# Attention and Fourier mixing on one core: start, last blocks and the turn of the row ends rearranged

## The chip, the core and the metric

The kernel runs on one core of one Trainium2 chip. The metric is the device time of one execution in microseconds (us), lower is better. Durations of single instructions come from a profile of one execution. In the profile PE is TensorE, PEld its weight loads, DVE is VectorE, ACT is ScalarE, POOL is GpSimd and SP is SyncE, which only issues DMAs here. A "q" behind an engine's name (SPq) marks its queue.

## What is computed

Two independent parts, laid side by side along the last axis of the output (2048 rows, 2 x 1024 columns, fp32):

```python
# A: attention with 32 heads of 32, one shared key and value head
q = (A_x @ wq) as [heads, rows, 32]; k = A_x @ wk; v = A_x @ wv
p = softmax(q @ k.T / sqrt(32)); a = concat_heads(p @ v) @ wo
# B: Fourier mixing, real part
re = B_x @ hid_re.T; im = B_x @ hid_im.T
b = seq_re @ re - seq_im @ im
out = concatenate([a, b], axis=-1)
```

The inputs have 2048 rows of 1024 columns, the sequence transform is 2048 x 2048. The inputs of A are scaled up, so that scores are large and the products must be precise.

## The kernel before

**Products in two parts.** Nearly every matrix product of 128 x 128 by 128 x 512 is done three times on operands rounded to fp32r: a left operand `m` is split into `mh` (rounded) and `ml` (the rest), a right operand `r` into `rh` and `rl`, and `rh*mh + rl*mh + rh*ml` is summed in PSUM. For each operand the steps are: load by SP, combine if it is a sum of several, round (`cast`, line 174), subtract the rounded part (`lo`, line 244). `cast` runs on ACT and the subtraction on DVE until the first 48 products are issued (`START`, line 563), later both on POOL. Two lines of such items, `RL` for right and `ML` for left operands (class `Line`, line 139; lines 257 and 258), have rings of buffers and due times counted in products: `pump` takes each step when the product it is due for is near, `step(k)` takes one step, `force(item)` takes all that an item still needs. A step of the program is an issue only; each engine works through its own queue in order, and waits where data or a buffer is not there.

**Fill.** A `Group` (line 77) is 24 such products (8 right blocks, 2 left items) into one PSUM bank named `psb`. `pos["fill"]` counts the products issued. `take(n)` (line 352) issues the next n. The groups are, in this order: the projections to q (32 groups, `q_group`), B's first stage, B's second stage (products as a scheme with fewer multiplications, so that operands are sums, `PRODUCTS`), and the output projection with wo. They are the "fill" that is put between the steps of attention, so that PE has work while ACT and DVE do the softmax.

**Attention.** 32 units (block of 512 rows times group of 4 heads). For each, 32 score steps (`score_step`, line 696): two products into a PSUM tile `pss` of 2 banks, DVE takes the negative row maximum into `nm`, ACT the exponential with its row sum. A unit's row ends are then formed in the next unit's first steps: `lse_1` (DVE, maxima), `lse_1b` (ACT, a small exponential), `lse_2` (DVE, sums and reciprocal), `lse_3` (PE turns the 48 columns of row ends into rows in a `psb` bank, DVE copies them to `mt`), `lse_4` (SP writes two rows into the unit's `qst` and one to memory). The table `LSE` and `TURN` (lines 712 and 713) say at which step. 12 steps behind, `expo` (line 655) forms the turned scores of the unit with these rows in the product, into PSUM tile `pst`, and ACT their exponential `p`; every eighth step `pv` (line 664) multiplies with the values in a `psb` bank.

**Order.** Every engine keeps the program's order (class `Ordered`), all DMAs go through SP's queue, and `level` (line 764) spreads the fill evenly over the 1024 steps from the point `PRO` that is reached after the opening.

**The opening** (lines 715 to 755). Three products of zeros (`v`, just cleared by DVE) into `pst`; then the first block of x: SP loads its 8 pieces, and behind the first of them ML's pump loads, rounds and subtracts the first two blocks of wq; then the 8 pieces of x are rounded and subtracted in turn. Keys and values are formed by `kv_pair` in fp32; `kst` holds the keys in three parts plus two rows of ones, and is cleared by two DVE memsets at lines 118 and 119. Between the two `kv_pair` and behind them stand three groups of fill (`take(24)` each), then the score steps begin, 7 products of fill behind each.

**The end** (lines 787 to 822). The last 8 groups are the last block of rows: for each the first 21 products (`first_part`), and the three with the last unit's result (`last_block`, line 337), which comes last. The first four groups have their 21 products done in the four halves of two `pss` tiles, then their last blocks in a row; the other four follow one by one in `psb`. Each group's `post` copies the bank with DVE into a buffer `qh` and `store` sends it to the output from SP's queue, `BEHIND` = 9 products later in program order.

[...]

Of the kernel before, what the change touches and what calls it, by code (L numbers as in the profile page):

```python
# [8 lines left out]
F32 = mybir.dt.float32  # L9
F32R = mybir.dt.float32r  # L10
AF = mybir.ActivationFunctionType
# [5 lines left out]
P = 128  # L17
# [4 lines left out]
W = 512  # L22
NG = 8
NQ = 4
# [63 lines left out]
def tile_kernel(ctx: ExitStack, tc, xT, wq, wkv, wo, xbT, wT, cT, out):  # L88
    nc = tc.nc
    te = Ordered(tc, nc.tensor)  # L90
    act = Ordered(tc, nc.scalar)
    dve = Ordered(tc, nc.vector)
    gp = Ordered(tc, nc.gpsimd)
    sp = Ordered(tc, nc.sync)
    scale = float(DH) ** -0.5

    def pool(stack, name, bufs, **kw):
        kw.setdefault("reuse_waits", "tile")
        return stack.enter_context(tc.tile_pool(name=name, bufs=bufs, **kw))
# [15 lines left out]
    kst = keep.tile([P, S], F32R, name="kst")  # L115
    v = keep.tile([P, NC, DH], F32, name="v")
    dve.memset(v, 0.0)
    dve.memset(kst[96:P, :].bitcast(F32), 0.0)
    dve.memset(kst[96:98, :].bitcast(F32), 1.0)

    ps_s = pool(ctx, "ps_s", 2, space=PSUM)
    ps_t = pool(ctx, "ps_t", 1, space=PSUM)
    ps_b = [pool(ctx, f"ps_b{i}", 1, space=PSUM) for i in range(2)]
# [8 lines left out]
    op = pool(ctx, "op", 3, side="right")  # L132
    hp = pool(ctx, "hp", 1, side="right")

    def move(q, to, of):
        q.dma_start(to.bitcast(F32), of.bitcast(F32))


    class Line:
# [22 lines left out]
        def pump(self):  # L162
            for k in range(4):
                while self.may(k) and self.items[self.n[k]].due - self.lead[k] <= pos["fill"]:
                    self.step(k)
# [92 lines left out]
    ML = Line(NM0, NM, (52, 36, 27, 21), load_m, comb, hi_m, lo)  # L258
# [42 lines left out]
    def at(p, f):  # L301
        k = len(later)
        while k and later[k - 1][0] > p:
            k -= 1
        later.insert(k, (p, f))

    def run_later():
        while later and later[0][0] <= pos["fill"]:
            later.pop(0)[1]()

    def soon(f):

        if pos["fill"] <= START:
            f()
        else:
            at(pos["fill"] + BEHIND, f)

    def store(to, of, key=None):
        def go():
            move(sp, to, of)  # L320
            if key:
                ready.add(key)
        soon(go)
# [4 lines left out]
    def bank(name, open_=False):  # L328

        b = 1 - cur["bank"] if cur["bank"] is not None else int(used[1] < used[0])  # L330
        cur["at"] += 1
        used[b] = cur["at"]
        if open_:
            cur["bank"] = b
        return ps_b[b].tile([P, W], F32, name=name)
# [10 lines left out]
    def product(g, ps, j):  # L346
        c, w = divmod(j, 3)
        l, r = g.left[c // 4], g.right[c]
        a = (l.lo if w == 2 else l.hi)[:, c % 4]
        te.matmul(ps[:g.rows], a, r.lo if w == 1 else r.hi, start=j == 0, stop=j == g.n - 1)  # L350

    def take(n):
        for _ in range(n):
            if cur["group"] >= len(groups):
                return
            g = groups[cur["group"]]
            j = pos["fill"] - g.at
            if j == 0:
                cur["ps"] = bank("psb", True)
            if j % 3 == 0:  # L360
                RL.force(g.right[j // 3])
            if j % 12 == 0:
                ML.force(g.left[j // 12])
            product(g, cur["ps"], j)
            pos["fill"] += 1
            if j == g.n - 1:
                cur["group"] += 1
                assert all(hasattr(it, "done") for it in g.ys)
                g.post(cur["ps"])
                cur["at"] += 1  # L370
                used[cur["bank"]] = cur["at"]
                cur["bank"] = None
                if g.ys:
                    at(pos["fill"] + 2 * BEHIND, lambda n=len(g.ys): yused.__setitem__(0, yused[0] + n))
            pump()
            run_later()
# [14 lines left out]
    def x_set(b):  # L391
        return [Item([(lambda c=c: xT[b, c], 1)]) for c in range(ND)]
# [148 lines left out]
    def o_left(b, t, q):  # L541
        g1 = min(q * 4 + 4, NQ * NG - 1 - b * NG)

        def src():
            assert all(("o", b, g) in ready for g in range(q * 4, g1)), (b, t, q)
            return [d[b][q * 4:g1, :, t * P:(t + 1) * P].rearrange("g p c -> p g c") for d in (oh_d, ol_d)]
        return Item(None, pre=src)

    def o_group(b, t, e, ws):
        def post(ps):  # L550
            oo = op.tile([P, W], F32, name="qh")
            dve.tensor_copy(oo, ps)
            r0 = b * W + t * P
            store(out[r0:r0 + P, e * W:(e + 1) * W], oo)
        return Group([o_left(b, t, q) for q in range(2)], ws, post)


# [3 lines left out]
    sets = [x_set(b) for b in range(NQ)]  # L561
    start = [q_group(0, g, sets[0]) for g in range(2)]
# [8 lines left out]
    pp = pool(ctx, "pp", 9)  # L571
# [62 lines left out]
    def lse_3(u):  # L634
        aside()
        pm = bank("psb")
        te.transpose(pm[:3 * NC, :P], nm[u][:, 3:6].rearrange("p a b -> p (a b)"), ident)
        mt = sm.tile([3 * NC, P], F32, name="mt")
        dve.tensor_copy(mt, pm[:3 * NC, :P])
        cur["at"] += 1  # L640
        lse[u] = mt
# [54 lines left out]
    def score_step(s):  # L696

        if s < total:
            u, r = divmod(s, SU)
            if r == SU - 6 and u + 1 < len(units):  # L700
                open_unit(u + 1)
        if SU <= s < SU * (len(units) + 1) and s % SU == TURN:
            lse_3((s - SU) // SU)
# [4 lines left out]
        if 0 <= u < len(units):  # L708
            for f in LSE.get(e, ()):
                f(u)  # L710

    TURN = 6
    LSE = {1: (lse_1,), 2: (lse_1b,), 4: (lse_2,), 8: (lse_4,)}

    zeros = v[:, :, :].rearrange("p a b -> p (a b)")
    for _ in range(3):
        te.matmul(ps_t.tile([P, 2, W], F32, name="pst")[:, 0], zeros[:, :P], zeros, start=True, stop=True)
    room = [t[:, k] for t in [pp.tile([P, 2, W], F32, name="p") for _ in range(9)] for k in range(2)]
    room += [hp.tile([P, W], F32, name=f"h{k}") for k in range(8)]
    room += [t[:, k].bitcast(F32) for t in [qsp.tile([P, 4, W], F32R, name="qst") for _ in range(2)] for k in range(4)]  # L720
# [2 lines left out]
    def load_x(b):  # L723
        for c in range(ND):
            sp.dma_start(xs[b][c], xT[b, c])
            if b < 2:
                sets[b][c].t = [xs[b][c]]
            if b == 0 and c == 0:
                ML.pump()

    load_x(0)
    for it in sets[0]:
        RL.force(it)
    wkv_t = onp.tile([P, W], F32, name="ov")
    sp.dma_start(wkv_t, wkv.rearrange("p a b -> p (a b)"))
# [8 lines left out]
    take(24)  # L744
    open_unit(0)
    kv_pair((2, 3), xs[2:])
    take(24)
    for s in range(SU + LEAD):
        score_step(s)
        take(7)  # L750
# [51 lines left out]
            pos["fill"] += 1  # L802
            pump()

    s0, s1 = (ps_s.tile([P, 2 * W], F32, name="pss") for _ in range(2))
    banks = [s0[:, :W], s0[:, W:], s1[:, :W], s1[:, W:]]
    for g, ps in zip(last[:4], banks):
        first_part(g, ps)
    for t, (g, ps) in enumerate(zip(last[:4], banks)):
# [2 lines left out]
        pump()  # L812
        run_later()
    for t, g in enumerate(last[4:]):
        ps = ps_b[t % 2].tile([P, W], F32, name="psb")
        first_part(g, ps)
        last_block(g, ps, t, hi7, lo7)
        pos["fill"] += 3
        pump()
        run_later()  # L820
# [36 lines left out]
```

## Time and profile before

| | us |
|---|---|
| median of three runs | 2773.06 (2770.75 to 2773.42) |
| the profiled execution | 2775.04 |
| its span, first to last instruction | 2773.1 |
| PE busy | 2756.9 (99%) |
| ACT busy | 2169.8 (78%) |
| POOL busy | 1648.2 (59%) |
| DVE busy | 1606.3 (58%) |

All instructions carry one line number, that of a helper, so they are told apart by the tiles they write and read (`out<-in`). A row of the timeline is: start, duration, engine, operation, tiles, shape, number of merged instructions, and in brackets the idle time of the engine just before and what ended it. The shown durations of products overlap, since they are pipelined; the distance from start to start tells the rate. "Granted clock" is the share of full speed that TensorE was given. A list of waits has: who waited, for whom, us in total, times, longest.

### The profile page before, as it was taken

The numbers are of one execution on the slowest core, as the hardware profiler recorded it, in microseconds if no ns is written. First come the engines' busy times: TensorE is split into PE (matmuls) and PEld (weight loads), VectorE is DVE, ScalarE is ACT, GpSimd is POOL, SyncE is SP. The second block draws the span as 40 slices with busy tenths as digits, with TensorE's granted clock in tenths as the row PEclk, the third lists the DMA queues.
The fourth block names the chain that finished last, engine by engine and source line by source line (L and its number), as shares of the span: only waits on it lengthen the run. The fifth ranks groups of instructions, "written<-read, shape, count | busy, mean of one in ns | idle before, by whom it ended". The sixth has DMA issues, their size and how long they took to land.

```text
span 2773.1 us, 39970 instructions
## 1 busy us (share of the span) xinstructions
PE 2756.9 (99%) x13870; PEld 1924.6 (69%) x13870; DVE 1606.3 (58%) x1836; ACT 2169.8 (78%) x3126; POOL 1648.2 (59%) x1618
## 2 busy tenths in 40 slices
PE   9999999999999999999999999999999999999999
PEld 6766676767767676776767676766776767676667
DVE  5766666666666665555556555555555555555411
ACT  3588888888888888888888888878888888888740
POOL 4755525666535547767786576798888885640110
PEclk9999999999999999999999999999999999999999
DMA  7544335675676555555463354565565552554455
GB/s 262 187 132 127 115 104 182 225 235 180 213 238 198 176 165 165 156 161 146 136 200 105 121 174 135 166 199 161 161 190 152 167 161 84 162 163 138 129 165 173
DMA packets 302329, 458.01 MB, mean 165 GB/s; under 512 B 31024, under 2 KB 96048, under 8 KB 302128
## 3 DMA queue, kind: packets, MB, share of 16 engines
q1 hardware_dynamic: 302128, 455.47, 52.8%
q8 instruction: 109, 1.79, 0.3%
q14 instruction: 92, 0.75, 0.1%
HBM read 349.44 MB, written 104.60 MB: 164 GB/s over the span
## 4 chain that ended last, share of the span: by engine, by line
PE 95%; DMA 2%; POOL 1%; DVE 1%; issue 1%; SPq 1%; ACT 0%; POOLq 0%; ACTq 0%
PE psb L66 60%; PE pss L66 18%; PE pst L66 17%; DMA r<-s 1%; DMA p<-in_xT_dram 1%; SPq L66 1%; POOL ml L66 0%; DMA m<-in_wq_dram 0%; DVE qh L66 0%; DMA h<-in_xT_dram 0%; DVE y L66 0%; ACT p L66 0%; ACT pss L66 0%; DVE nm L66 0%; POOL mh L66 0%
## 5 line engine op out<-in xcount | busy, mean ns | idle before, releaser
L66 DVE TENSOR_REDUCE nm<-pss 128x1 f32<-128x1024 f32 x1024 | 1252.9, 1224 | 598.8 <-PE pss L66 598.2
L66 ACT ACTIVATE p<-pst 128x1024 f32<-128x1024 f32 x1024 | 1052.1, 1027 | 463.8 <-PE pst L66 461.0
L66 ACT ACTIVATE pss<-pss,nm 128x1024 f32<-128x1024 f32 x1024 | 1110.7, 1085 | 59.4 <-DVE nm L66 57.6
L66 PE MATMUL psb<-rh,ml 128*128 128x512 f32 x1820 | 716.7, 394 | 4.4 <-POOL ml L66 4.4
L66 PE MATMUL psb<-rh,mh 128*128 128x512 f32 x1820 | 716.7, 394 | 0.5 <-DVE y L66 0.4
L66 PE MATMUL psb<-rl,mh 128*128 128x512 f32 x1820 | 714.6, 393 | 0.5 <-DVE rl L66 0.5
L66 PE MATMUL pss<-kst,qst 128*128 128x512 f32 x2048 | 657.7, 402 | 2.4 <-DMA kst<-qh 2.4
L66 PE MATMUL pst<-qst,kst 128*128 128x512 f32 x2048 | 648.5, 397 | 1.1 <-ACT p L66 1.0
L66 PEld LDWEIGHTS pss<-kst,qst 128*128 128x128 f32 x2048 | 372.4, 188 | 186.1 <-issue 99.8
L66 PE MATMUL psb<-p,v 128*32 128x512 f32 x4096 | 467.1, 596 | 0.0
L66 POOL TENSOR_TENSOR ml<-m,mh 128x512 fp32r<-128x512 f32 x338 | 437.1, 1293 | 37.8 <-ACT mh L66 30.0
L66 PEld LDWEIGHTS pst<-qst,kst 128*128 128x128 f32 x2048 | 378.1, 188 | 106.8 <-ACT p L66 18.5
L66 PEld LDWEIGHTS psb<-rh,ml 128*128 128x128 f32 x1820 | 341.9, 188 | 86.1 <-POOL ml L66 6.1
L66 PEld LDWEIGHTS psb<-rh,mh 128*128 128x128 f32 x1820 | 341.8, 188 | 85.3 <-issue 1.2
L66 PEld LDWEIGHTS psb<-rl,mh 128*128 128x128 f32 x1820 | 341.8, 188 | 80.5 <-DVE rl L66 0.8
L66 POOL TENSOR_TENSOR r<-r,r 128x512 f32<-128x512 f32 x112 | 144.6, 1291 | 282.6 <-DMA r<-s 154.6
L66 PEld LDWEIGHTS psb<-p,v 128*32 128x32 f32 x4096 | 120.1, 110 | 277.2 <-issue 265.1
L66 POOL CAST mh<-m 128x512 fp32r<-128x512 f32 x337 | 207.0, 614 | 150.5 <-PE psb L66 132.3
L66 POOL CAST rh<-r 128x512 fp32r<-128x512 f32 x208 | 128.2, 617 | 263.2 <-PE psb L66 147.0
L66 POOL TENSOR_TENSOR rl<-r,rh 128x512 fp32r<-128x512 f32 x208 | 269.0, 1294 | 3.8
L66 POOL TENSOR_TENSOR m<-m,m 128x512 f32<-128x512 f32 x192 | 248.3, 1293 | 29.3 <-DMA m<-in_xbT_dram 23.9
L66 DVE TENSOR_TENSOR ov<-ov,psb 128x512 f32<-128x512 f32 x96 | 66.0, 688 | 270.5 <-PE psb L66 270.5
(75 smaller groups left out, 940.8 us busy)
## 6 DMA issues: line engine op xcount, KB each, us to landing
m<-in_cT_dram SPq DMA_DIRECT2D x384, 256.0 KB, 3.7
r<-s SPq DMA_DIRECT2D x192, 256.0 KB, 4.4
y<-y SPq DMA_DIRECT2D x96, 256.0 KB, 4.6
r<-in_wT_dram SPq DMA_DIRECT2D x80, 256.0 KB, 3.7
m<-in_xbT_dram SPq DMA_DIRECT2D x80, 256.0 KB, 4.3
y<-u SPq DMA_DIRECT2D x80, 256.0 KB, 2.9
m<-in_wq_dram SPq DMA_DIRECT2D x64, 256.0 KB, 3.1
qst<-qh SPq DMA_DIRECT2D x64, 256.0 KB, 5.7
```

Source lines behind the costliest of these rows:

```text
L66: return lambda *a, **k: self.tc.keep_in_program_order(f(*a, **k))
```

## The change

- The two memsets of `kst` go from DVE to POOL.
- The products of zeros become two instead of three, of 512 and of 384 columns.
- In the opening the first wq block is loaded behind the first piece of x and the second behind the second. Rounding begins with wq's first block, then two pieces of x, then wq's second block, then the rest of x. Before it was both blocks of wq, then x.
- 48 products of fill instead of 24 stand behind the second `kv_pair`, in front of the first scores.
- `TURN` goes from 6 to 4, and the steps of `LSE` from 1, 2, 4, 8 to 0, 1, 2, 5.
- The last eight groups take five PSUM tiles in turn (two `pss`, `pst`, two `psb`), one group in each.
- The copies of the last eight groups alternate between ACT and DVE, into buffers of `p`, and are sent at once from ACT's queue; the last group's copy and store are cut in two halves of 256 columns, one copied by ACT and sent from ACT's queue, one copied by DVE and sent from SP's.

```diff
-    dve.memset(kst[96:P, :].bitcast(F32), 0.0)
-    dve.memset(kst[96:98, :].bitcast(F32), 1.0)
+    gp.memset(kst[96:P, :].bitcast(F32), 0.0)
+    gp.memset(kst[96:98, :].bitcast(F32), 1.0)
...
+    halves = []
+
     def o_group(b, t, e, ws):
         def post(ps):
-            oo = op.tile([P, W], F32, name="qh")
-            dve.tensor_copy(oo, ps)
             r0 = b * W + t * P
-            store(out[r0:r0 + P, e * W:(e + 1) * W], oo)
+            to = out[r0:r0 + P, e * W:(e + 1) * W]
+            if b < NQ - 1:
+                oo = op.tile([P, W], F32, name="qh")
+                dve.tensor_copy(oo, ps)
+                store(to, oo)
+                return
+
+            n = len(halves)
+            halves.append(n)
+            oo = pp.tile([P, 2, W], F32, name="p")
+            if n + 1 < 8:
+                if n % 2:
+                    dve.tensor_copy(oo[:, 0], ps)
+                else:
+                    act.activation(oo[:, 0], ps, AF.Copy)
+                move(act, to, oo[:, 0])
+                return
+            for k, q in enumerate((act, sp)):
+                cols = slice(k * W // 2, (k + 1) * W // 2)
+                if k:
+                    dve.tensor_copy(oo[:, k, :W // 2], ps[:, cols])
+                else:
+                    act.activation(oo[:, k, :W // 2], ps[:, cols], AF.Copy)
+                move(q, to[:, cols], oo[:, k, :W // 2])
...
-    TURN = 6
-    LSE = {1: (lse_1,), 2: (lse_1b,), 4: (lse_2,), 8: (lse_4,)}
+    TURN = 4
+    LSE = {0: (lse_1,), 1: (lse_1b,), 2: (lse_2,), 5: (lse_4,)}
...
-    for _ in range(3):
-        te.matmul(ps_t.tile([P, 2, W], F32, name="pst")[:, 0], zeros[:, :P], zeros, start=True, stop=True)
+    for n in (W, 3 * P):
+        te.matmul(ps_t.tile([P, 2, W], F32, name="pst")[:, 0, :n], zeros[:, :P], zeros[:, :n], start=True, stop=True)
...
-            if b == 0 and c == 0:
-                ML.pump()
+            if b == 0 and c < 2:
+                ML.step(0)
 
     load_x(0)
-    for it in sets[0]:
+    for n, it in enumerate(sets[0]):
+        if n % 2 == 0 and n < 4:
+            ML.force(start[0].left[n // 2])
         RL.force(it)
...
     kv_pair((2, 3), xs[2:])
-    take(24)
+    take(48)
...
-    s0, s1 = (ps_s.tile([P, 2 * W], F32, name="pss") for _ in range(2))
-    banks = [s0[:, :W], s0[:, W:], s1[:, :W], s1[:, W:]]
+    def whole(i):
+        if i % 5 < 2:
+            return ps_s.tile([P, 2 * W], F32, name="pss")[:, :W]
+        if i % 5 == 2:
+            return ps_t.tile([P, 2, W], F32, name="pst")[:, 0]
+        return ps_b[i % 5 - 3].tile([P, W], F32, name="psb")
+
+    banks = [whole(i) for i in (0, 1, 2, 3)]
...
-        ps = ps_b[t % 2].tile([P, W], F32, name="psb")
+        ps = whole(4 + t)
```

## The prediction

> **What bounds the kernel now.** First the stretches of the run, then what TensorE waited for, then the places in order of time. In the stretches, the columns are length, busy time of PE, weight loads, DVE, ACT and POOL (instructions in brackets), granted clock, DMA share, GB/s.
>
> ```profile
> 7.00:13.30 6.30, 5.84 (x24) 4.35 (x24) 5.05 (x9) 4.13 (x7) 0.00 (x0) 1.00 1.05 383
> ...
> 40.00:47.00 7.00, 4.95 (x15) 3.93 (x16) 3.19 (x4) 1.21 (x2) 4.01 (x5) 0.76 0.92 256
> 135.00:1780.00 1645.00, 1643.46 (x8359) 1144.28 (x8358) 1011.76 (x1154) 1368.19 (x1976) 992.07 (x973) 1.00 0.52 164
> 1780.00:1860.00 80.00, 75.61 (x374) 51.09 (x377) 43.61 (x49) 63.65 (x93) 71.94 (x68) 0.98 0.67 212
> 2712.00:2774.00 62.00, 55.49 (x257) 42.55 (x256) 9.42 (x14) 1.03 (x1) 3.75 (x4) 1.00 0.55 167
> ```
>
> ```profile
> PE psb L66 <- POOL ml L66: 4.4, 4, 1.8
> PE pss L66 <- DMA kst<-qh: 2.4, 1, 2.4
> PE pss L66 <- DVE qh L66: 1.6, 2, 0.8
> ```
>
> PE is the bound nearly everywhere: 1643.46 us busy of 1645 in the long middle stretch. The change leaves PE's real work alone, so it can only touch what PE loses: at the start, in front of the first scores (2.4 us waiting, and a clock of 0.76 over 7 us), in the last blocks (1.6 us), and around 1780 to 1860 (4.4 us, POOL), which no edit aims at.
>
> **The change part by part.** *Start* (shorter warm-up, the two memsets of kst on POOL, first operands rounded in another order). The rows:
>
> ```profile
> 1.46 5.39 PE L66 MATMUL pst<-v 128*128 128x512 f32 x6 [1.46 <-DVE v L66]
> ...
> 4.14 1.76 DVE L66 MEMSET kst<- 2x2048 f32 x1 [0.48 <-DVE kst L66]
> 4.16 0.63 ACT L66 ACTIVATE mh<-m 128x512 fp32r<-128x512 f32 x1 [2.13 <-DMA m<-in_wq_dram]
> ...
> 5.72 0.63 ACT L66 ACTIVATE mh<-m 128x512 fp32r<-128x512 f32 x1 [0.94 <-DMA m<-in_wq_dram]
> 5.94 1.29 DVE L66 TENSOR_TENSOR ml<-m,mh 128x512 fp32r<-128x512 f32 x2
> 6.26 4.95 ACT L66 ACTIVATE rh<-p 128x512 fp32r<-128x512 f32 x8
> ...
> 6.93 0.49 PE L66 MATMUL psb<-rh,mh 128*128 128x512 f32 x1
> 7.15 4.90 DVE L66 TENSOR_TENSOR rl<-p,rh 128x512 fp32r<-128x512 f32 x8
> ...
> 13.00 0.39 PE L66 MATMUL psb<-rh,ml 128*128 128x512 f32 x1
> ```
>
> Today ACT rounds both blocks of wq (4.16 and 5.72, the second after its DMA) before the first x (6.26), DVE is held by the memset until 5.90, and the three warm-up products end at 6.85. In the new order the first x is rounded right behind the first wq block: 4.16 + 0.63 + 0.63 = 5.42. The warm-up is (512 + 384)/512 of a product instead of three; a slow one takes about 2.1 us by estimate (three in 5.39 us, the last at the higher rate), so it ends near 1.46 + 2.1 + 1.6 = 5.2. The first real product starts at about 5.45 instead of 6.93.
>
> Of these 1.5 us most is lost again to the loads. In 7.00:13.30 the DMAs move 383 GB/s at a share of 1.05, so 256 KB take 0.68 us, and the chain of waits shows how long a load takes in that queue:
>
> ```profile
> 3.55 5.03 DMA p<-in_xT_dram
> ```
>
> The load issued at 3.55 is the seventh of ten (eight of x, two of wq) and lands at 8.58; the tenth lands near 8.58 + 3 x 0.68 = 10.6. ACT (0.63) and DVE (0.69) follow: the last rl is there at about 12.0, whatever came before. The last two products of the group then start at 12.0 and 12.2, and the group ends at 12.45 to 12.6, against 13.00 + 0.23 = 13.23 now. **Gain 0.7 us**; bounds 1.5 (the loads hide) and -0.9 (the clock drops, a rival below). POOL's two memsets of 1.76 us cost nothing: POOL has no instruction at all in 7.00:13.30. Without that cover they would still be over long before kst is read at 42.05 (next rows). DVE's queue loses two instructions and no DMA is added; the second wq load is issued one place later on SP, behind a load of x that is wanted earlier.
>
> *More fill in front of the first scores.* Here 24 more products, the whole fourth group, move ahead of score step 0.
>
> ```profile
> 36.87 1.29 POOL L66 TENSOR_TENSOR ml<-m,mh 128x512 fp32r<-128x512 f32 x1
> ...
> 39.31 0.39 PE L66 MATMUL psb<-rh,ml 128*128 128x512 f32 x1
> 39.84 0.59 SPq L66 DMA_DIRECT2D kst<-y  x1
> ...
> 42.05 0.70 PE L66 MATMUL pss<-kst,qst 128*128 128x512 f32 x2 [2.35 <-DMA kst<-qh]
> ...
> 44.20 0.63 PE L66 MATMUL psb<-rh,ml 128*128 128x512 f32 x1
> 44.63 0.63 PE L66 MATMUL psb<-rh,mh 128*128 128x512 f32 x1
> ```
>
> PE is free at 39.31 + 0.23 = 39.54 and starts the scores at 42.05: 2.51 us lost. Then products start 0.43 us apart instead of 0.23, and the clock of 0.76 over 7 us is worth 0.24 x 7 = 1.68 us. Together **4.2 us**. With the fill, PE reaches that place at 38.8 and works 24 x 0.23 = 5.5 us, to 44.3 (0.23 a product: the four steps from 2744.07 to 2745.00, in the rows of the last blocks below, take 0.93). Are its operands there? The group's second left block is done on POOL at 36.87 + 1.29 = 38.16 and wanted at 38.8 + 12 x 0.23 = 41.6; its right operands are those of the first group. What the scores wait for comes meanwhile. The DMA issues give, as their last column, the median time to landing:
>
> ```profile
> kst<-y SPq DMA_DIRECT2D x4, 64.0 KB, 3.8
> ```
>
> So the last piece of kst, issued at 39.84, lands at about 43.6, 0.7 us before 44.3. Bounds: 0 to 4.2; I take 4.2 because both covers hold by the rows. Later PE is 24 products further in the list; the planner spreads the rest over 1024 steps, 0.02 of some 5 products in a step, at no cost and with less rather than more load on POOL in 1780:1860.
>
> [...]
>
> *Last blocks in five PSUM tiles, turned copies, halves.*
>
> ```profile
> 2742.55 0.40 PE L66 MATMUL pss<-rh,ol 128*128 128x512 f32 x1
> 2742.98 0.69 DVE L66 COPY qh<-pss 128x512 f32<-128x512 f32 x1 [19.05 <-PE pss L66]
> 2743.73 0.50 PE L66 MATMUL pss<-rh,oh 128*128 128x512 f32 x1 [0.78 <-DVE qh L66]
> 2744.07 0.39 PE L66 MATMUL pss<-rl,oh 128*128 128x512 f32 x1
> ...
> 2745.00 0.40 PE L66 MATMUL pss<-rh,ol 128*128 128x512 f32 x1
> 2746.18 0.50 PE L66 MATMUL pss<-rh,oh 128*128 128x512 f32 x1 [0.78 <-DVE qh L66]
> ...
> 2768.66 0.40 PE L66 MATMUL psb<-rh,ol 128*128 128x512 f32 x1
> 2769.10 0.69 DVE L66 COPY qh<-psb 128x512 f32<-128x512 f32 x1 [4.79 <-PE psb L66]
> 2769.82 0.33 SPq L66 DMA_DIRECT2D out_dram<-qh  x1
> ```
>
> Two of the four blocks share a PSUM tile with the one before, and PE waits for that one's copy: from start to start 1.18 us instead of 0.23, twice, and the product after each starts 0.34 later, not 0.23. 2 x (0.95 + 0.11) = **2.1 us**. With a tile each, the four blocks run through, and a tile comes round again five groups later. The copies alternate ACT and DVE and all but the last group's second half are sent from ACT's queue, where only one other instruction stands in the whole stretch (1.03 us, x1, the last exponential); behind a DMA that waits for DVE only the next copy is queued, 5 us ahead of need. SP loses the stores that stood between its loads.
>
> At the very end one copy of 0.69 and a store become two halves on two engines and queues. ACT and DVE do not read one PSUM tile side by side here:
>
> ```profile
> 20.48 0.60 ACT L66 ACTIVATE y<-pss 128x512 f32<-128x512 f32 x1 [0.32 <-PE pss L66]
> 21.11 0.69 DVE L66 CAST qh<-pss 128x512 fp32r<-128x512 f32 x1 [0.23 <-ACT y L66]
> ```
>
> DVE, idle, waited for ACT's read. Half a copy is about 0.36 on ACT (0.60 for 512 columns, 1.03 for the 1024 of the last exponential) and 0.42 on DVE (0.28 for 128 columns in the copy of mt below, 0.69 for 512). One after the other they take 0.8, so the second half leaves 0.1 later than now, with half the bytes (at most 0.34 us less). Side by side it would gain up to 0.6. I take **0.1**, bounds -0.2 and 0.6.
>
> *Rows' ends turned and sent sooner.* The transposition of a unit's row ends moves from score step 6 to 4, its reductions from steps 1, 2, 4 to 0, 1, 2, its three small DMAs on SP from 8 to 5.
>
> ```profile
> 1002.71 1.23 DVE L66 TENSOR_REDUCE nm<-pss 128x1 f32<-128x1024 f32 x1 [0.81 <-PE pss L66]
> 1004.57 1.23 DVE L66 TENSOR_REDUCE nm<-pss 128x1 f32<-128x1024 f32 x1 [0.63 <-PE pss L66]
> ...
> 1006.43 0.25 DVE L66 RECIPROCAL nm<-l 128x16 f32<-128x16 f32 x1
> ...
> 1011.69 0.28 DVE L66 COPY mt<-psb 48x128 f32<-48x128 f32 x1 [0.74 <-PE psb L66]
> ```
>
> DVE needs 1006.68 - 1004.57 = 2.1 us from the reduction of the step to the reciprocal; the turn comes two steps of about 1.9 us (1002.71 to 1004.57) after that step's scores, and these lie some 0.3 us in front of the reduction, so about 3.5 us after it: 1.4 us are to spare, 0.7 if a group's copy of 0.69 stands between. Behind the turn PE has scores and exponentials (two pairs of products, 0.9 us), then the value products, which take the same PSUM tile and wait for the copy of 0.28. It fits, and PE waits for nothing of this today either. On SP the three DMAs pass the loads of three steps; SP is in front of PE, and now a step with a block of value products lies between turn and issue instead of two steps without. **Cost 0**, bounds 0 and 1.
>
> **Sum.** 0.7 + 4.2 + 2.1 + 0.1 = 7.1 us. The profiled execution took 2775.04 us, 2773.1 of them in its span: it becomes 2767.9, with a span of 2766.0. The median of the runs shown is 2773.06, 2 us below the profiled one; taken off it, the forecast is **2766.0 us**.
>
> **The rivals.**
> 1. *The clock drops at the start.* From 5.45 to about 9 PE works as the loads land: every 0.68 us or more an x that gives three products of 0.23, in the mean, so it may be idle for some 1.6 us of 3.5, in pauses of about 0.5. Pauses of 0.95 in the last blocks left the clock at 1.00, for it; the sum of idle time is near that of the pause of 1.8, against it. A drop as the one at 43 costs 1.6 us: 2767.6.
> 2. *The clock is not won back:* the pause is not what lowers it, or the timed runs lose it elsewhere, or not before either. 7.1 - 1.7 = 5.4 us, 2767.7. The 2.7 us between fastest and slowest run speak for drops that come and go, the row of 0.76 right behind the pause against. [...]
> 3. *The stall only moves:* the fourth group or the scores wait for an operand as long as before. 2.9 us are left, 2770.2. The margins of 3.3 and 0.7 us speak against it.
> 4. *The stretch at 1780 changes too.* POOL is 90% busy there, and where a unit's own work falls decides the 4.4 us and the 0.02 x 80 = 1.6 us of clock. Up to 4 us less, 2762; or 2 more.
> 5. *Slower: the turn makes PE wait in each of 32 units.* If the row ends come later than the turn, every unit pays. From 7.1/32 = 0.22 us each the gain is gone, and with 0.6 us (a group's copy and a reduction in front) it is 32 x 0.6 = 19 us: 2778. The spare 0.7 us speak against it.
>
> That the edit doesn't do what it says is rival 3.
>
> **How the numbers follow.** Forecast 0.50; rival 1 0.17; 2 0.12; 3 0.06; 4 0.11; 5 0.04. The range runs from 2763.0 (rival 4 in part, halves side by side) to 2769.5 (rivals 1 and 2 together, with 2 us more at 1780). A measurement of this kernel can tell about 0.2% from no change, 5.5 us, so below 2767.5 counts as faster: the forecast, most of 4 and about half of 1 and 2 (they lie at the bound), 0.72. Same: the other half, 3 and a little of 4, 0.24. Slower 0.04.
>
> **What would show it.** Right: the first real product near 5.45 and the first group's last near 12.3; no wait of PE on kst, the scores starting near 44.3, clock 1.00 in 40:47; last blocks 0.23 us apart; PE's waits on POOL about 4.4. Wrong: a granted clock under 1 in the first 15 us, a wait for ml or kst near 40, or a new line of PE waiting for DVE's reciprocal or mt, with a count near 32.

## The result, and the profile after

| | before | after |
|---|---|---|
| median, us (11 runs each) | 2773.06 (2770.75 to 2775.30) | 2765.83 (2764.38 to 2768.01) |
| the profiled execution | 2775.04 | 2764.96 |
| its span | 2773.1 | 2762.9 |

The time falls by 7.2 us, to 0.9973 of before [0.9965, 0.9982]. The two profiled executions lie further apart, 10.1 us, and where the other 3 come from is a question for the experiments.

The stretches of the changed kernel come first, columns as before:

```profile
7.00:13.30 6.30, 5.85 (x24) 3.70 (x24) 4.64 (x7) 3.79 (x6) 0.00 (x0) 1.00 1.05 398
...
40.00:47.00 7.00, 7.00 (x33) 5.73 (x32) 2.88 (x5) 0.00 (x0) 4.28 (x6) 1.00 0.91 265
135.00:1780.00 1645.00, 1643.36 (x8365) 1148.59 (x8364) 1013.95 (x1156) 1373.76 (x1983) 993.70 (x975) 1.00 0.52 165
1780.00:1860.00 80.00, 76.31 (x390) 51.87 (x389) 43.48 (x50) 62.93 (x91) 70.76 (x66) 1.00 0.64 198
```

Then all that PE waited for in it (us in total, times, longest):

```profile
PE psb L66 <- POOL ml L66: 3.7, 4, 1.2
PE pst L66 <- DVE v L66: 1.5, 1, 1.5
PE psb L66 <- DVE y L66: 0.8, 2, 0.5
PE psb L66 <- DVE rl L66: 0.8, 3, 0.3
PE pst L66 <- ACT p L66: 0.7, 3, 0.3
PE psb L66 <- ACT rh L66: 0.4, 1, 0.4
```

PE is busy all 7 us of 40 to 47 (4.95 before), with 33 products instead of 15, and the clock there is 1.00. The waits for `kst` and for DVE's `qh` are gone, and no new one has come near a count of 32. The timeline around the first scores and at the end of the changed kernel:

```profile
44.62 0.40 PE L66 MATMUL psb<-rh,ml 128*128 128x512 f32 x1
44.85 0.62 PE L66 MATMUL pss<-kst,qst 128*128 128x512 f32 x2
```

```profile
2734.57 0.40 PE L66 MATMUL pss<-rh,ol 128*128 128x512 f32 x1
2734.80 0.40 PE L66 MATMUL pss<-rh,oh 128*128 128x512 f32 x1
...
2735.27 0.40 PE L66 MATMUL pss<-rh,ol 128*128 128x512 f32 x1
2735.50 0.40 PE L66 MATMUL pst<-rh,oh 128*128 128x512 f32 x1
...
2758.57 0.40 PE L66 MATMUL pst<-rh,ol 128*128 128x512 f32 x1
2759.01 0.38 ACT L66 ACTIVATE p<-pst 128x256 f32<-128x256 f32 x1 [4.88 <-PE pst L66]
...
2759.43 0.42 DVE L66 COPY p<-pst 128x256 f32<-128x256 f32 x1 [10.62 <-ACT p L66]
2759.88 0.35 SPq L66 DMA_DIRECT2D out_dram<-p  x1
```

The scores follow the fill in 0.23 us without a wait. In the last blocks the first product of a block follows the last of the one before in 0.23 us, where it took 1.18. The two halves of the last copy run one after the other (0.38 and 0.42 us; DVE, idle for 10.62, starts behind ACT).

**Where the time went.** The start of a score step is a mark that both kernels have. What the changed kernel had gained by then is the difference of the two starts, plus 0.2277 us for each product of fill that one has issued more than the other (worked out from the starts of all products in the two traces):

| up to | gained, us | in this part |
|---|---|---|
| end of the first group | 0.15 | 0.15 |
| score step 0 | 2.66 | 2.51, the pause |
| step 32 | 4.30 | 1.64, the clock |
| step 704 (near 1780 us) | 5.74 | 1.44 |
| step 736 (near 1860 us) | 8.02 | 2.28 |
| step 1023 | 7.99 | -0.03 |
| end of the span | 10.24 | 2.25, the last blocks and the halves |

Pause, clock and last blocks give 6.4 us and are the forecast's terms. The opening gives 0.15 instead of 0.7. Two parts, 1.44 and 2.28 us, stand in no term of the sum. Some 1.7 of the 2.28 are a second drop of the clock in the execution of the kernel before, from 1855.67 on; the changed kernel's has none there.

### The profile page after: what moved, and what is told of

It is laid out like the page before. It is cut to its first block, busy times and chain, and to the rows that moved or that the text cites. A ratio compares the mean times of both kernels' runs of the same rounds, so it can differ in the third digit from the quotient of the medians.

```text
span 2762.9 us, 39957 instructions
## 1 busy us (share of the span) xinstructions
PE 2750.9 (100%) x13868; PEld 1927.0 (70%) x13868; DVE 1599.3 (58%) x1830; ACT 2173.0 (79%) x3131; POOL 1650.2 (60%) x1620
## 4 chain that ended last, share of the span: by engine, by line
PE 97%; POOL 1%; DMA 1%; DVE 1%; issue 0%; ACT 0%; SPq 0%; POOLq 0%; ACTq 0%; DVEq 0%
PE psb L66 60%; PE pss L66 19%; PE pst L66 17%; POOL y L66 0%; DVE nm L66 0%; SPq L66 0%; DMA u<-y 0%; DVE y L66 0%; ACT p L66 0%; DMA p<-in_xT_dram 0%; POOL ml L66 0%; DMA m<-in_cT_dram 0%; DMA r<-s 0%; ACT pss L66 0%; POOL rl L66 0%
```

## The experiments

The theory: the 7.2 us are the fill (some 4.2) and the last blocks (2.2), the opening and the turn are worth nothing, and the stretch at 1780 differs from one execution to the next. Rivals: the opening carries some of it; the pause isn't what lowers the clock; the turn acts through the stretch at 1780. The last runs ask what bounds that stretch. "Changed" is the changed kernel, "before" the kernel before; gains from traces are counted as in the table above. Each ratio is to runs of the kernel before on the same chip.

### The fill

**Undone alone** (changed):

```diff
-    take(48)
+    take(24)
```

> The changed kernel with 24 instead of 48 products in front of the first scores. My theory (the fill covers a pause of 2.5 us and thereby saves the clock drop behind it, 1.7 us): the wait on kst comes back with about 2.4 us, the granted clock in 40 to 47 us falls below 0.85, and the time is 4.2 us above the changed kernel's, about 2770.0. Rival (the clock drop is not tied to this pause): the wait comes back, the clock stays at 1.00, 2.5 us above, 2768.3. Rival (the stall only moves): no difference, 2765.8.

Measured: 2771.78 us, 0.9996 [0.9987, 1.0005]: nearly all of the gain is gone, 6.4 us by the two ratios (some 3 us either way) where 4.2 were expected. Neither the wait of 2.4 us nor a clock below 0.85 shows in its profile: in this execution the first group ended 1.9 us later than before (the clock, see the opening), so PE came later to the pause and waited 0.3 us for `kst` only:

```profile
40.00:47.00 7.00, 6.70 (x32) 5.19 (x31) 4.40 (x7) 2.21 (x3) 4.62 (x6) 1.00 0.88 248
```

What follows: without the fill, time lost in the opening is taken out of the pause (1.92 us behind the kernel before at the end of the first group, 0.13 ahead of it at score step 0). The mean granted clock that is on record for each run is below 1.000 in all 11 of these runs, in 5 of them 0.998, so each lost time to the clock somewhere, in the profile from 1852.67 on; whether that is all that goes beyond the 4.2 is not shown.

**Done alone** (before):

```diff
-    take(24)
+    take(48)
```

> The kernel before with one edit: 48 instead of 24 products in front of the first scores. My theory (the fill takes the pause of 2.5 us and with it the clock drop of 1.7 us): no wait on kst, clock 1.00 in 40 to 47 us, 4.2 us below the kernel before, about 2768.7. Rival (the clock is not won back): 2.5 us below, 2770.3, with a granted clock under 1 somewhere in the first 60 us. Rival (what the changed kernel without the fill showed, 1 us below the kernel before, means that the fill is worth 6 us): 6 us below, 2766.8.

Measured: 2769.62 us against 2773.74, 0.9982 [0.9974, 0.9991], 4.1 us less. The same stretch, without a wait for `kst`:

```profile
40.00:47.00 7.00, 7.00 (x32) 5.74 (x31) 2.75 (x5) 0.00 (x0) 4.00 (x6) 1.00 0.90 218
```

This is the term of 4.2, measured by itself.

**The pause filled with work that is worth nothing** (before). Two more products like those of the warm-up go behind the third group; they add no result (`zeros` is the tile `v`, which holds values by then):

```diff
     take(24)
+    for _ in range(2):
+        te.matmul(ps_t.tile([P, 2, W], F32, name="pst")[:, 0], zeros[:, :P], zeros, start=True, stop=True)
```

> The kernel before with two products of zeros (about 1.07 us each, results not used) put where the fill was added, so that PE is kept busy in the pause without doing any of its work. My theory (the pause itself lowers the clock): the scores start at about 42.1 as before, PE waits no more than 0.5 us, the clock is 1.00 in 40 to 47 us, and the time is 1.7 us below the kernel before, about 2771.1. Rival (the drop has nothing to do with the pause): the clock falls below 0.85 there all the same, and the time is the same, 2772.8.

Measured: 2773.22 us against 2773.74, 0.9996 [0.9987, 1.0005], an interval that holds both 0 and the 1.7 us of the clock, so the time tells nothing. The trace does. What is left to wait for, and the stretch:

```profile
PE pss L66 <- DMA qst<-qh: 0.8, 2, 0.6
```

```profile
40.00:47.00 7.00, 6.70 (x26) 4.40 (x25) 3.69 (x5) 2.12 (x3) 4.24 (x5) 1.00 0.89 248
```

The scores start when they did (42.01), so the pause itself is not won; but the clock is 1.00 instead of 0.76, and at step 32 this execution is 1.62 us ahead. That standing still is what lowers the clock does not follow from one execution, since the clock stayed at 1.00 behind a pause of 2.1 us too (the opening alone, below); the part on the prediction sets the pauses of several traces side by side.

### The opening

**Undone alone** (changed): DVE's memsets, three whole warm-up products, the old order of loads and rounding:

```diff
...
-    for n in (W, 3 * P):
+    for n in (W, W, W):
...
-            if b == 0 and c < 2:
-                ML.step(0)
+            if b == 0 and c == 0:
+                ML.pump()
...
```

> The changed kernel with the opening of before: three products of zeros, the memsets of kst on DVE, both blocks of wq rounded ahead of x. My prediction's term (0.7 us): 2766.5, the first group's last product 0.7 us later than the changed kernel's 12.85. What the trace of the changed kernel says (0.15 us): 2766.0, the last product at about 13.0. Both: the first real product comes near 6.9 instead of 5.63, and the loads decide the end of the group.

Measured: 2764.64 us, 0.9971 [0.9960, 0.9981], no slower than with the new opening (0.9973). Its first group ends 0.26 us later than the changed kernel's.

**Only the warm-up undone** (changed):

```diff
-    for n in (W, 3 * P):
+    for n in (W, W, W):
```

> The changed kernel with three products of zeros of 512 columns again, in the new order of rounding. Theory (with the shorter warm-up PE's first products can fall into the slow clock, which then lasts beyond 9 us; seen in three of four profiles with the short one): the clock is at 1.00 from 8 us at the latest, the first real product at about 6.9, the first group's last product about 1.9 us behind the landing of the last x, and the time up to 1 us below the changed kernel's, 2764.8 to 2765.8. Rival (the shorter warm-up gains): the group ends later, 2766.5.

Measured: 2765.64 us, 0.9972 [0.9960, 0.9983]. No difference either.

**Done alone** (before), the opening's edits without the others:

```diff
...
-    for _ in range(3):
+    for n in (W, 3 * P):
...
-            if b == 0 and c == 0:
-                ML.pump()
+            if b == 0 and c < 2:
+                ML.step(0)
...
```

> The kernel before with the changed opening alone (shorter warm-up, memsets on POOL, new order of rounding). My theory (without the fill everything up to 42 us is hidden by the wait for the first unit's q and the keys): no difference to the kernel before, 2773.0 to 2773.7, the scores start at 42.0 whatever the first group does. Rival (the opening's gain of up to 0.7 us goes through): 0.7 us below. Rival (a late clock at the start makes the opening a loss): 1 to 2 us above.

Measured: 2772.33 us against 2772.49, 1.0000 [0.9991, 1.0008]. Its wait and its stretch:

```profile
PE pss L66 <- DMA kst<-qh: 2.1, 1, 2.1
```

```profile
40.00:47.00 7.00, 5.26 (x23) 4.31 (x24) 3.88 (x5) 2.38 (x4) 4.32 (x5) 1.00 0.79 243
```

Without the fill the wait for `kst` stands nearly as before (2.4 us). In this profile the first group ends only 0.04 us earlier than before, so there was nothing to hide; that the wait takes up what the opening does is seen in the run without the fill above. Of note: 2.1 us of waiting left the clock at 1.00 here.

**The changed kernel again**, nothing edited, to see how far one execution's profile stands for it:

> The changed kernel again, unchanged, beside the other three: 2765.8, and the spread of its clock at the start. Theory of the opening (the warm-up of 3.8 us is about as long as what the clock needs, so the clock reaches 1.00 either near 5.5 us or only after 9 us): one or the other, not between 6 and 8.5 us.

Measured: 2764.74 us (2763.78 to 2767.89), 0.9972 [0.9963, 0.9982]; the profiled execution is the slowest of its ten, 2767.89. Its opening on PE:

```profile
5.37 0.79 PE L66 MATMUL psb<-rh,mh 128*128 128x512 f32 x1
...
12.94 0.63 PE L66 MATMUL psb<-rh,ml 128*128 128x512 f32 x1
13.37 0.63 PE L66 MATMUL psb<-rh,mh 128*128 128x512 f32 x1
...
14.42 0.39 PE L66 MATMUL psb<-rh,mh 128*128 128x512 f32 x1
14.65 0.39 PE L66 MATMUL psb<-rl,mh 128*128 128x512 f32 x1
...
15.55 0.39 PE L66 MATMUL psb<-rh,ml 128*128 128x512 f32 x1
```

and beside it the opening of the first profile of the same program:

```profile
1.46 3.78 PE L66 MATMUL pst<-v 128*128 128x512 f32 x4 [1.46 <-DVE v L66]
...
5.63 0.50 PE L66 MATMUL psb<-rh,mh 128*128 128x512 f32 x1 [0.38 <-ACT rh L66]
...
8.31 3.30 ACT L66 ACTIVATE rh<-p 128x512 fp32r<-128x512 f32 x5 [0.55 <-DMA p<-in_xT_dram]
...
12.85 0.39 PE L66 MATMUL psb<-rh,ml 128*128 128x512 f32 x1
```

In the one the products stand 0.43 us apart until 14, in the other 0.23 from the start. The first group ends 2.7 us later, and that is almost the whole difference of the spans (2765.9 and 2762.9). The distance of the products shows this. The granted clock of the stretches reads 1.00 there in both, because the trace's clock records begin only with the higher rate (14.13 and 5.26 us), and time without a record counts as 1.00. The moment from which the products run at the higher rate, for all profiles by their warm-up:

| warm-up | higher rate from, us | last product of the first group, us |
|---|---|---|
| short (8 profiles) | 5.3, 5.7, 9.0, 9.9, 10.1, 10.2, 12.9, 14.1 | 12.85, 12.90, 12.62, 12.96, 13.33, 13.08, 14.92, 15.55 |
| three products (6 profiles) | 5.1, 5.6, 5.8, 6.1, 7.5, 7.8 | 13.39, 13.00, 13.60, 13.03, 13.29, 13.11 |

With three products the first group's last product starts at 13.24 in the mean. The short warm-up lies between 0.6 us before that and 0.1 behind when the rate rises by 10.2, and some 2 us behind when it rises after that: 13.53 in the mean of its eight profiles.

### The turn of the row ends

**Undone alone** (changed):

```diff
-    TURN = 4
-    LSE = {0: (lse_1,), 1: (lse_1b,), 2: (lse_2,), 5: (lse_4,)}
+    TURN = 6
+    LSE = {1: (lse_1,), 2: (lse_1b,), 4: (lse_2,), 8: (lse_4,)}
```

> The changed kernel with the row ends turned at step 6 and sent at step 8, as before. My theory (the turn is off PE's path): within 0.5 us of the changed kernel's 2765.8, and PE's waits on POOL around 1780 to 1860 stay near 3.7 us. Rival (the turn gave what the trace shows beyond the sum, 1.4 us between steps 64 and 704 and 2.3 us between steps 704 and 736): 1.4 to 3.7 us above, 2767.2 to 2769.5.

Measured: 2766.59 us, 0.9978 [0.9969, 0.9987], not to be told from the changed kernel. In the trace one wait appears that neither the kernel before nor the changed one showed:

```profile
PE pst L66 <- DMA qst<-mt: 2.2, 1, 2.2
```

It falls at 1829 us, where SP is late (see the stretch at 1780). The run with the fill alone, also with the old turn, has it too (2.7 us, once). So the earlier turn costs nothing, and takes a wait out of reach that the fill can bring. Between steps 32 and 704 seven of the nine profiles with the new turn gained 1.3 to 1.5 us on the kernel before (one 0.8, and one, with POOL's work moved, lost 0.2), and the four with the old turn -0.8 to 0.4. That this is the turn's doing is not shown, but it fits: a gain of about 1 us, 0.05 in each of 21 units, too small for the time to show. The granted clock of the runs shows more: with 48 products of fill and the old turn (this run and the fill alone) it is below 1.000 in 12 of 21 runs, so each of these 12 had at least one drop of the clock; with 48 and the new turn (seven kernels, the changed one among them) it is in 5 of 65.

### The last blocks

**Undone alone** (changed): the tiles as before, copies and halves as after:

```diff
-    banks = [whole(i) for i in (0, 1, 2, 3)]
+    s0, s1 = (ps_s.tile([P, 2 * W], F32, name="pss") for _ in range(2))
+    banks = [s0[:, :W], s0[:, W:], s1[:, :W], s1[:, W:]]
...
-        ps = whole(4 + t)
+        ps = ps_b[t % 2].tile([P, W], F32, name="psb")
```

> The changed kernel with the last blocks of the first four groups in halves of two PSUM tiles again, the other four in psb in turn; copies and queues stay as changed. My theory (a shared tile makes PE wait for the neighbour's copy): two waits of PE of about 0.8 us each come back, 2.1 us above, 2767.9. Rival (the gain of the last blocks came from sending the copies sooner and from two engines): no waits, 2765.8.

Measured: 2767.22 us, 0.9982 [0.9973, 0.9991] (changed 0.9973): the right side, a difference that the time alone doesn't resolve. In the trace the two waits are back, now for ACT's copies:

```profile
PE pss L66 <- ACT p L66: 1.9, 2, 1.2
```

From step 1023 to the end it loses 0.2 us to the kernel before, and the changed kernel gains 2.25: 2.4 us for the tiles.

### The stretch at 1780

The changed kernel's profile gains 2.28 us there, with 3.7 us of waits for POOL's `ml` and no drop of the clock; the kernel before had 4.4 and 0.98. The profiles of the twelve experiments show 0 to 5.5 us of that wait. Two theories for it: POOL has too much work (70.76 us of 80), or POOL itself waits. In the changed kernel, what POOL waited for between 1780 and 1870, what SP waited for on POOL between 1795 and 1830, then POOL's and SP's timelines:

```profile
POOL r L66 <- DMA r<-s: 9.3, 5, 4.9
```

```profile
SPq L66 <- POOL ml L66: 19.1, 5, 4.8
```

```profile
1811.11 1.28 POOL L66 TENSOR_TENSOR ml<-m,mh 128x512 fp32r<-128x512 f32 x1
...
1817.91 1.29 POOL L66 TENSOR_TENSOR ml<-m,mh 128x512 fp32r<-128x512 f32 x1
1820.92 1.29 POOL L66 TENSOR_TENSOR r<-r,r 128x512 f32<-128x512 f32 x1 [1.72 <-DMA r<-s]
```

```profile
1812.42 0.81 SPq L66 DMA_DIRECT2D m<-in_cT_dram  x2
1813.27 0.91 SPq L66 DMA_DIRECT2D y<-y  x2
1814.28 1.15 SPq L66 DMA_DIRECT2D qst<-mt  x2
1815.47 0.58 SPq L66 DMA_DIRECT2D r<-mt  x1
1816.09 0.90 SPq L66 DMA_DIRECT2D r<-s  x2
1819.23 0.81 SPq L66 DMA_DIRECT2D m<-in_cT_dram  x2
```

SP loads `m` the moment POOL is done with an old one (1811.11 + 1.28 = 1812.39, then 1812.42; again 1817.91 + 1.29 = 1819.20, then 1819.23). The load of `r` is queued behind it, goes out at 1816.09 to 1816.99, and POOL stands still until 1820.92 to use it. POOL waits for a load that SP could not send because SP was waiting for POOL.

**Less work for POOL** (changed): the three last steps of each attention unit (multiply, round, subtract) on DVE, where only the last unit's are so far:

```diff
-            e = dve if last else gp
+            e = dve
```

> The changed kernel with the three last steps of each unit (multiply, round, subtract: 1.3 + 0.6 + 1.3 us on POOL) on DVE for all units, where only the last unit has them so far. My theory (the stretch 1780 to 1860 is bound by POOL): PE's waits on POOL's ml fall from 3.7 to under 1.5 us, and the time is 2 to 3 us below the changed kernel's, about 2763.3, if DVE's 1.8 us more a unit hold up nothing. Rival (the loads of r bound it): the waits stay, 2765.8. Rival (DVE delays the score reductions): a new wait of PE on ACT or DVE in each unit, above 2766.

Measured: 2766.44 us, 0.9974 [0.9965, 0.9984]. POOL's work between 135 and 1780 fell from 993.70 to 942.81 us, and PE's wait stayed:

```profile
PE psb L66 <- POOL ml L66: 3.5, 4, 1.1
```

That speaks against the theory that POOL has too much work. It does not settle it: between 1780 and 1860 POOL was busy for 70.44 us, almost as before, although DVE took over work there (46.88 instead of 43.48). The next run does.

**The loads of `r` sent earlier** (changed): all loads of right operands are issued 64 instead of 40 products ahead, so in SP's order they move in front of the loads of `m` that wait:

```diff
-    RL = Line(NR0, NR, (40, 40, 14, 8), load_r, comb, hi_r, lo)
+    RL = Line(NR0, NR, (64, 40, 14, 8), load_r, comb, hi_r, lo)
```

> The changed kernel with the loads of right operands issued 64 instead of 40 products ahead. Theory (around 1780 to 1860 POOL idles until r<-s lands, because SP comes to these loads late, behind loads of m that wait for POOL): POOL's waits on r<-s there fall from 9.3 to under 3 us, PE's waits on POOL's ml from 3.7 to under 1.5 us, and the time is 2 to 3 us below the changed kernel's, about 2763.3. Rival (POOL has too much work there, 71 of 80 us): PE's waits stay between 3 and 5 us, 2765.8.

Measured: 2761.10 us (2760.74 to 2761.68), 0.9959 [0.9947, 0.9972]. The stretch, and all of PE's waits in the whole span:

```profile
1780.00:1860.00 80.00, 80.00 (x411) 55.96 (x410) 46.71 (x52) 67.08 (x98) 78.75 (x75) 1.00 0.71 223
```

```profile
PE pst L66 <- DVE v L66: 1.5, 1, 1.5
PE psb L66 <- DVE y L66: 0.8, 2, 0.5
PE pst L66 <- ACT p L66: 0.7, 3, 0.3
```

PE is busy 80 of 80 us, and POOL 78.75 of 80 instead of 70.76: it had room to work more all along. Neither POOL's wait for `r<-s` nor PE's for `ml` is left. SP waits for POOL's `ml` nearly as long as before (18.2 us between 1795 and 1830), but the loads of `r` no longer stand behind such a wait. That they did was the cause.

**The same with the old opening** (changed, the rest of the opening undone as above):

```diff
...
-    RL = Line(NR0, NR, (40, 40, 14, 8), load_r, comb, hi_r, lo)
+    RL = Line(NR0, NR, (64, 40, 14, 8), load_r, comb, hi_r, lo)
...
-    for n in (W, 3 * P):
+    for n in (W, W, W):
...
```

> The changed kernel with the loads of right operands 64 products ahead and with the opening of before. If the opening's edits are worth nothing (the loads decide the end of the first group) and the earlier loads 2.5 us: the same as with the earlier loads alone, about 2763.3, and the fastest so far. If the new opening is worth its 0.7 us: 2764.0. If the earlier loads do nothing: 2765 to 2766.

Measured: 2760.82 us (2760.68 to 2761.33), 0.9959 [0.9946, 0.9971]. It is the fastest of all, but the same as the one above within the runs; all its runs lie below all of the changed kernel's on the same chip (2763.78 to 2767.89). With and without the new opening the time is the same once more.

## Why the prediction was right, and where not

**The total** was forecast at 7.1 us and is 7.2. That agreement is better than its terms, and so in part luck: the opening gives less than its 0.7, the clock is lost in only about half of the executions of the kernel before (40 of 75, below), and what makes up for both was in no term. The upper end of the range is added up wrongly: rivals 1 and 2 together with 2 us more are 2766.0 + 1.6 + 1.7 + 2 = 2771.3, not 2769.5.

**More fill, 4.2: right in its mechanism; the part of the clock depends on the execution.** It is 4.1 us alone by time (2.5 to 7.2 by the ratio's interval), and 2.51 and 1.64 in the traces. The scores started at 44.85 (forecast 44.3) without a wait. Rival 3 (the stall only moves) falls with PE's list of waits.

What the scores had waited for is not what the prediction took it for. Score step 0 reads only the first half of the keys, whose last piece lands at 34.25 in the trace of the kernel before; the pieces issued up to 39.84 are for step 1. In all four profiles in which PE waited there, step 0 starts 0.13 to 0.14 us behind the landing of the first unit's `qst`, as in the run with the two added products (a row of its chain of waits: start, us, what):

```profile
36.20 5.68 DMA qst<-qh
```

It landed at 41.88, and the scores started at 42.01; the list of waits of the kernel before names `kst` for the same wait. In the changed kernel this load lands at 42.18, so the fill covers it with 2.7 us to spare, where the prediction had counted on 0.7.

Rival 2 (the clock isn't won back) falls at this place: 1.00 in 40 to 47 with the fill, and with the two added products too. Two of its cases hold in part. The clock can be lost elsewhere: the profile of the fill alone has a drop from 1834.60 on, behind the wait for `qst<-mt`. And about half of the timed runs do not lose it before either. A drop of 3.4 us to half the rate takes 0.0006 off the mean granted clock of a run. Of the 75 runs of the kernel before that were timed beside the experiments, 35 read 1.000, which leaves no room for a drop; the other 40 took 1.7 to 2.2 us longer in the mean, on each of the three chips. Of the changed kernel's 21 runs with a clock on record 18 read 1.000. By estimate the clock is therefore worth (40/75 - 3/21) x 1.7, or 0.7 us, in the mean, wherever in the run its drops lie, and not the 1.68 of the sum. The 4.1 us of the fill alone agree with that only within their interval.

Not every pause was followed by a drop, and the length of the pause does not tell which: behind 2.4 us in front of the first scores the clock fell in the kernel before (0.76 in 40 to 47). Two pauses near 1850, the first of the kernel before, the second of the changed kernel with the old turn:

```profile
1854.30 0.49 PE L66 MATMUL psb<-rh,ml 128*128 128x512 f32 x1 [1.83 <-POOL ml L66]
```

```profile
1829.60 0.70 PE L66 MATMUL pst<-qst,kst 128*128 128x512 f32 x2 [2.25 <-DMA qst<-mt]
```

Behind the one of 1.83 us the clock fell (the 0.98 of its stretch; the products run 0.43 apart for 3.4 us from 1855.7), and behind the one of 2.25 it stayed at 1.00, as behind the 2.1 of the opening alone.

The clock records of the traces, from which the column of the granted clock is formed, show more. In the kernel before the two drops last 3.413 us each, and the stretches at full speed in front of them 37.547 and 1809.064 us, 11 and 530 times as long. So its trace can be cut into slices of 3.413 us that begin and end with the records, and the time without a product in each can be counted. First the slice in front of the drop at 43.20 in the kernel before, then the two slices, cut in the same way, that the pause of the opening alone lies in, columns as before:

```profile
39.79:43.20 3.41, 1.15 (x5) 1.01 (x6) 1.74 (x3) 0.00 (x0) 1.44 (x2) 1.00 0.99 234
```

```profile
37.19:40.60 3.41, 2.47 (x13) 1.71 (x11) 1.36 (x4) 0.00 (x0) 3.33 (x4) 1.00 1.07 249
40.60:44.02 3.42, 2.28 (x10) 1.91 (x11) 1.74 (x2) 0.28 (x1) 0.74 (x2) 1.00 0.80 225
```

In the first PE stands still for 3.41 - 1.15 = 2.26 us. In the other two, counted alike, it is 0.94 and 1.14 us. So it is near 1850: the pause of 1.83 us lies in one slice, the one in front of the drop at 1855.67, and the pause of 2.25 in two (0.93 and 1.31). Up to the last product no other slice of the kernel before has more than 1.38 us without a product, and none of the changed kernel's, which has no drop, more than 1.22. In two more traces with a drop near 1850 the 3.41 us in front of it hold 1.83 us of pause (the fill alone, 1831.19 to 1833.02) and 3.15 (the fill undone, 1849.26 to 1852.41). One slice does not fit in: 1.88 us without a product at the end of the opening alone, and no drop behind it. The author's reading is that standing still lowers the clock, and that it depends on how a pause of 2 us lies to the slices, which differs from one execution to the next, whether it costs 1.7 us (3.41 at half the rate) more. These counts agree with it; what in the chip would do so they do not show.

**Five PSUM tiles, 2.1, and the halves, 0.1: right.** 2.25 us together in the trace, 2.4 for the tiles alone against the old tiles. The halves ran one after the other (ACT from 2759.01 for 0.38 us, DVE from 2759.43), as the row of 20.48 said. From the last product's start to the last landing it takes 3.23 us instead of 3.39, worked out from the traces.

**The turn, 0: right** as a cost. Rival 5 falls: no wait with a count near 32. (Its 2778 should be 2766.0 + 19.2 = 2785.) That SP's small loads come earlier is even of use: with the fill and the old turn 12 of 21 runs hold a drop of the clock, about as many as in the kernel before (40 of 75), with the new turn 5 of 65. So the 0.7 us of the clock come from the fill and the turn together.

**The opening, 0.7: wrong in size.** The step that failed is "the first group ends at 12.45 to 12.6". It took the tenth load to land at 10.6, and the last products to follow its rounding. In the rows of the changed kernel's opening, ACT's last rounding starts at 11.61 - 0.63 = 10.98, so that load landed some 0.35 later (in the profiles it lands between 10.4 and 11.8); and PE, held up by earlier pieces, worked off a queue of products 0.23 apart from 10.30 to the end, another 0.25. That leaves 0.15. Nor is it the same in each execution: rival 1, the clock at the start, is real and was given 0.17. It isn't a drop, as the rival said, but a rate that rises late, at 9 to 14 us in six of eight profiles with the short warm-up; the sign that was named for it, a granted clock under 1 in the first 15 us, cannot show it, since there are no clock records before the rise. It costs 2 us only when it rises after some 10 us, in two of the eight; where it rises sooner, the loads hide most of it. By time the opening is worth nothing measurable (three comparisons: undone, done alone, and with the lead of 64).

**The stretch at 1780: rival 4, in part.** It came out 2.28 us better in the profile of after, some 1.7 of it the second drop of the clock in the profile of before, and explains most of why the two profiled executions differ by 10 us while the medians differ by 7: without it and the 1.44 us of drift the traces give 6.5. That the change itself improves the stretch is not shown: in the second profile of the same program, and in the runs with one part undone, it gained between -0.5 and 4.4. What bounds it is shown (the loads of `r` behind loads that wait for POOL); that the clock drops there in some executions only (0.98 in 1780 to 1860 in three of the fourteen profiles, 1.00 in the others) is part of why it differs so much from run to run, and the rest stays open. The drift of 1.44 between steps 32 and 704 stays open too.

## What to carry to other kernels

Fill in front of a stall on data was worth the stall here (2.51 us in the traces), and in those executions in which the clock fell behind the stall the clock too (1.64). An edit that only makes the work in front of a standing stall shorter can be worth nothing: without the fill, 1.92 us lost in the opening were gone at the first scores. When an engine looks like the bound at nearly 90% busy, look at what it waits for itself: here loads stood in one in-order queue behind others that waited for the same engine, POOL stood still for 9.3 us to wait for them, and issuing them earlier gave 3.6 us more (2764.74 to 2761.10 on one chip). Two profiled executions of the same program lay 3 us apart here (spans of 2762.9 and 2765.9), in places that no edit touched, so terms of this size are settled by a trace mark for mark, and by runs.

## What the runs showed of the hardware that was not expected

With the warm-up of 3.78 us the higher rate came at 5.3 to 14.1 us, at 9 or later in six of eight profiles. With three products (5.39 us) it came by 7.8 in all six. In the kernel before it came at 5.65, and from there to the first drop at 43.20 it is 37.55 us, 11 times the 3.413 us that the drop lasts. Until the first rise the granted clock of the stretches reads 1.00 although the products run at the low rate; only the distance between them tells (0.43 us or 0.23).
